# The last chunk of a two-layer kernel cut by groups instead of by tiles, and its last stores on two queues

## The chip, the cores and the metric

The kernel runs on one core of a Trainium2 chip. The metric is the device time of one execution in microseconds (us). The engines are PE (matrix multiply; PEld is its weight load), DVE (vector), ACT (activation), POOL (general purpose) and SP, which here only issues DMAs. ACT can issue DMAs too.

## What is computed

An attention over 12480 tokens of 128 channels with 32 inducing points, and then two layers of 128 to 2048 to 128, the first with `h * cos(h)`, the second with `h * sigmoid(h)`:

```python
h = mab(I, x)                       # 32 points attend to all tokens
x = mab(x, h)                       # all tokens attend to the 32 points
h = x @ w_in;  x = (h * np.cos(h)) @ w_out      # first layer
h = x @ w_in2; out = (h / (1 + np.exp(-h))) @ w_out2   # second layer
```

## The kernel before, in words

The 12480 tokens are seen as 98 tiles: tile t holds for each of 128 partitions one token, and the last tile (t = 97) holds 64 tokens only. The 128 partitions of a tile are four groups g of 32. A run of nt tiles of one group is therefore nt * 32 columns of a matmul; tile 97 exists for groups 0 and 1 alone, so that groups 2 and 3 have 32 columns less there (`width`, L198).

The tiles are cut into seven chunks (L71 to L73): 8 tiles, five times 16 tiles, and the last 10 tiles (88 to 97). The attention of a chunk is done at once; then the chunk's columns are cut into blocks of at most 512 columns (L264 to L272). A full chunk gives four blocks, one group with 16 tiles each. The first and the last chunk are cut by tiles instead: a block takes four tiles (MT) of all four groups. The last chunk thus gives blocks of 512, 512 and 192 columns. There are NB = 25 blocks.

A block goes through both layers in NJ = 8 units; a unit is 256 of the 2048 hidden channels. The kernel has one loop over steps s (L977), written as a software pipeline by hand; step s does for different units:

- `mlp1_in(s)`: 2 matmuls into the PSUM buffer h1 (L768). ACT takes the cosine (L797), DVE multiplies (L801), rounds (L808) and takes the rest (L819).
- `mlp2_in(s - 11)`: 6 matmuls into the single PSUM buffer h2 (L877). ACT does Silu (L892) and rounds (L900), POOL takes the rest (L901). In the last three units the halves of the rounding and of the rest are shared between DVE, ACT and POOL (L903 to L908).
- `mlp2_out(s - 13)`: 6 matmuls (L829) that add up in acc2. After the eighth unit of a block `store` (L921) turns the result on DVE (L924) into the single buffer o and issues its stores on SP (L933, L939).
- `mlp1_out(s - 2)`: 6 matmuls (L829) that add up in acc1; after the eighth unit `y_split` (L857) rounds it on ACT (L862) and takes the rest on DVE (L863).

So a unit costs PE 20 matmuls, whatever the number of its columns. Instructions are issued in the order of the program (a manual schedule), each engine takes its own in that order, and after the last `mlp1_in` 13 more steps drain the pipeline.

`spread` (L289) loads a block's attention weights with DMAs on SP into `stk`: four DMAs for each run of tiles of one group, eight steps ahead of the block. `store` issues for each such run four stores (32 channels each), and one more for a tail tile of groups 0 and 1. A block of one group has one run, a block cut by tiles has four. The last block (tiles 96 and 97 of all groups, 192 columns) thus has 16 stores at L933 and two at L939, in the order: four of group 0, tail of group 0, four of group 1, tail of group 1, four of group 2, four of group 3.

Of the kernel before, what the change touches and what calls it, by code (L numbers as in the profile page):

```python
# [21 lines left out]
def tile_induced_attention_then_two_mlps(  # L22
# [31 lines left out]
    nc = tc.nc  # L54
# [11 lines left out]
    KT = 16  # L66
# [197 lines left out]
    blocks, first_of = [], []  # L264
    for k, (t0, nt) in enumerate(chunks):
        first_of.append(len(blocks))
        if nt == KT:
            blocks += [(k, [(g, t0, nt)]) for g in range(G)]
        else:
            for t in range(t0, t0 + nt, MT):  # L270
                m = min(MT, t0 + nt - t)
                blocks.append((k, [(g, t, m) for g in range(G)]))  # L272
    NB = len(blocks)
# [3 lines left out]
    def places(b):  # L277

        at, out = 0, []
        for g, t, m in blocks[b][1]:  # L280
            n = width((t, m), g)
            out.append((g, t, m, at, n))
            at += n
        return out

    def cols(b):
        return sum(n for *_, n in places(b))
# [459 lines left out]
    def main(general):  # L747
# [173 lines left out]
        def store(b):  # L921
            n = cols(b)
            o = blk.tile([P, KT, Q], F32, tag="o", name="o", bufs=1)
            nc.vector.transpose(  # L924
                o.rearrange("p t d -> p (t d)")[:, 0:n], acc2.pop(b)[:, 0:n]
            )
            ov = out[0 : TF * P, :].rearrange("(p t) c -> p t c", t=TF)
            for g, t, m, at, _ in places(b):
                at //= Q
                full = min(t + m, TF) - t  # L930
                for d in range(G):
                    ds = slice(d * Q, (d + 1) * Q)
                    nc.sync.dma_start(  # L933
                        out=ov[g * Q : (g + 1) * Q, t : t + full, ds],
                        in_=o[ds, at : at + full, :],
                    )
                if full < m and g < GT:
                    r0 = TF * P + g * Q
                    nc.sync.dma_start(  # L939
                        out=out[r0 : r0 + Q, :].rearrange("i (d j) -> d i j", d=G),  # L940
                        in_=o[:, at + full, :],
                    )
# [34 lines left out]
        for s in range(NU + L2 + D2 + 1):  # L977
            if s < NU:
                mlp1_in(s)
            v = s - L2  # L980
            if 0 <= v < NU:
                mlp2_in(v)
            if s < L2:
                out1(s)
            if s < NU:
                mlp1_act(s)
            attend(s, True)
            if 0 <= v < NU:
                mlp2_act(v)
            v = s - L2 - D2  # L990
            if 0 <= v < NU:
                mlp2_out(v)
                if v % NJ == NJ - 1:
                    store(v // NJ)
            if s < NU:
                mlp1_rest(s)
            if s >= L2:
                out1(s)
            attend(s, False)
            more = wait_words or wait_sign or wait_join  # L1000
            if s >= L2:
                words()
            splits(1, 1 if more else 0)
            if s >= PAIRS and wait_pair:
                split(*wait_pair.pop(0))
            fill(s)
# [42 lines left out]
```

## Time and profile before

| | us |
|---|---|
| median of 3 runs | 1006.42 |
| lowest and highest | 1004.85, 1007.32 |
| the profiled execution | 1007.78 |
| its span (first to last instruction) | 1005.9 |

The time of the profiled execution is the span and what lies around it. Starts and lengths in the views are us from the start of the span. A matmul's length holds its way through the array, and matmuls overlap: what a matmul costs in a stream is the distance from one to the next. A row of the chain of waits that merges several matmuls gives such a stream's length. "Granted clock" is the share of TensorE's full clock of 2.4 GHz; 0.5 of it is 1.2 GHz.

### The profile page before, as it was taken

To read this page: it belongs to the slowest core of one execution; us is meant where nothing else is said; L and a number is where in the kernel's file an instruction comes from. 1 tells how busy PE (TensorE), PEld (TensorE's weight loads), DVE (VectorE), ACT (ScalarE), POOL (GpSimd) and SP (SyncE) were. 2 spreads that over 40 slices of the span, in tenths; PEclk is the share of its full clock that TensorE was granted. 3 is DMA by queue.
4 is the path that set the end of the run, shared out by engine and by line. 5 is a ranking of instruction groups with operands and counts; after the bars stand their busy time and mean duration, and the time that the engine had idled before them with its cause. 6 is when DMAs were issued, how large, how long until landed. Compare 5 with 4: busy or idle time off the path is not lost.

```text
span 1005.9 us, 12280 instructions
## 1 busy us (share of the span) xinstructions
PE 972.1 (97%) x4527; PEld 765.3 (76%) x4527; DVE 777.3 (77%) x817; ACT 704.0 (70%) x785; POOL 511.5 (51%) x285
## 2 busy tenths in 40 slices
PE   9987999999999999999999999999999999999993
PEld 6644577788887788887788887788887888888883
DVE  4876588888888888888888888888888888888520
ACT  5778676776766777676777676776767777767662
POOL 2234355555455555555564545555554655454572
PEclk9999999999999999999999999999999999999997
DMA  8431010110010010010010010010010010000001
GB/s 284 131 115 53 22 21 1 21 33 5 17 22 5 16 22 10 13 22 10 11 22 11 12 22 9 12 22 11 11 22 11 11 19 14 11 15 11 1 11 18
DMA packets 67788, 27.93 MB, mean 28 GB/s; under 512 B 55848, under 2 KB 61704, under 8 KB 67720
## 3 DMA queue, kind: packets, MB, share of 16 engines
q1 hardware_dynamic: 67672, 27.06, 11.2%
q8 instruction: 37, 0.61, 0.2%
q14 instruction: 31, 0.25, 0.1%
q10 hardware_dynamic: 48, 0.02, 0.0%
HBM read 14.79 MB, written 6.39 MB: 21 GB/s over the span
## 4 chain that ended last, share of the span: by engine, by line
PE 87%; ACT 3%; DVE 2%; issue 2%; POOL 1%; POOLq 0%; DVEq 0%
PE acc L829 49%; PE h L877 26%; PE h L768 8%; PE acc L839 2%; ACT c L797 1%; ACT L892 1%; ACT s L892 1%; PE s L215 1%; DVE c L801 0%; DVE s2t L226 0%; ACT s2t L236 0%; PE hwps L657 0%; DVE sign L137 0%; DVE sign L132 0%; ACT L236 0%
## 5 line engine op out<-in xcount | busy, mean ns | idle before, releaser
L901 POOL TENSOR_TENSOR lo<-s,hi 128x1024 fp32r<-128x1024 f32 (+1 forms) x189 | 447.4, 2367 | 391.5 <-ACT hi L900 343.7
L829 PE MATMUL acc<-hi,wo 128*128 128x512 f32 (+1 forms) x1504 | 401.6, 389 | 0.2 <-DVE o L924 0.2
L797 ACT ACTIVATE c<-h,half_pi 128x1024 f32<-128x1024 f32 (+1 forms) x200 | 219.0, 1095 | 160.4 <-PE h L768 160.1
L829 PEld LDWEIGHTS acc<-hi,wo 128*128 128x128 f32 x1504 | 279.3, 188 | 60.1 <-issue 1.4
L801 DVE TENSOR_TENSOR h<-h,c 128x1024 f32<-128x1024 f32 (+1 forms) x184 | 221.3, 1203 | 134.2 <-ACT c L797 134.1
L877 PE MATMUL h<-yhi,wi 128*128 128x512 f32 (+1 forms) x800 | 246.5, 390 | 6.3 <-ACT s L892 5.6
L892 ACT ACTIVATE s<-h 128x1024 f32<-128x1024 f32 (+1 forms) x200 | 201.0, 1005 | 69.5 <-PE h L877 67.0
L829 PE MATMUL acc<-lo,wo 128*128 128x512 f32 (+1 forms) x752 | 230.7, 388 | 0.0
L808 DVE CAST hi<-h 128x1024 fp32r<-128x1024 f32 (+1 forms) x184 | 220.0, 1196 | 6.3
L819 DVE TENSOR_TENSOR lo<-h,hi 128x1024 fp32r<-128x1024 f32 (+1 forms) x184 | 219.0, 1190 | 5.5
L900 ACT CAST hi<-s 128x1024 fp32r<-128x1024 f32 (+1 forms) x189 | 195.6, 1035 | 6.1
L877 PEld LDWEIGHTS h<-yhi,wi 128*128 128x128 f32 x800 | 147.6, 188 | 42.4 <-ACT s L892 8.6
L829 PEld LDWEIGHTS acc<-lo,wo 128*128 128x128 f32 x752 | 140.4, 188 | 31.7
L877 PE MATMUL h<-ylo,wi 128*128 128x512 f32 (+1 forms) x400 | 154.8, 387 | 0.0
L768 PE MATMUL h<-stk,hw 128*128 128x512 f32 (+1 forms) x400 | 127.7, 401 | 7.4 <-DVE c L801 6.8
L768 PEld LDWEIGHTS h<-stk,hw 128*128 128x128 f32 x400 | 74.3, 189 | 36.5 <-DVE c L801 12.2
L877 PEld LDWEIGHTS h<-ylo,wi 128*128 128x128 f32 x400 | 75.2, 188 | 15.9
L801 DVE TENSOR_TENSOR c<-h,c 128x1024 f32<-128x1024 f32 x16 | 19.6, 1222 | 19.9 <-ACT c L797 17.8
L839 PE MATMUL acc<-c,wf 128*128 128x512 f32 x64 | 31.2, 612 | 0.9 <-DVE ylo L863 0.9
L863 DVE TENSOR_TENSOR ylo<-acc,yhi 128x512 fp32r<-128x512 f32 (+1 forms) x25 | 16.8, 671 | 12.6 <-ACT yhi L862 12.5
L862 ACT CAST yhi<-acc 128x512 fp32r<-128x512 f32 (+1 forms) x25 | 14.4, 576 | 16.2 <-PE acc L829 13.1
L924 DVE STREAM_TRANSPOSE o<-acc 128x512 f32<-128x512 f32 (+1 forms) x25 | 17.3, 694 | 8.1 <-PE acc L829 8.1
(138 smaller groups left out, 365.8 us busy)
## 6 DMA issues: line engine op xcount, KB each, us to landing
x_sb<-in_x_dram SPq DMA_DIRECT2D x10, 512.0 KB, 6.4
out_dram<-o SPq DMA_DIRECT2D x80, 64.0 KB, 2.0
raw<-in_moe_w_in_dram SPq DMA_DIRECT2D x16, 256.0 KB, 3.3
raw<-in_moe_w_out_dram SPq DMA_DIRECT2D x16, 256.0 KB, 2.8
stk<-ahi SPq DMA_DIRECT2D x40, 64.0 KB, 2.0
stk<-at SPq DMA_DIRECT2D x40, 64.0 KB, 2.0
out_dram<-o SPq DMA_DIRECT2D x66, 16.0 KB, 1.5
x_sb<-in_x_dram SPq DMA_DIRECT2D x3, 192.0 KB, 5.9
```

What stands on the lines that cost most here:

```text
L768: nc.tensor.matmul(ps[:, a, 0:n], lhsT=hw[f // 4][:, f % 4 * P : (f % 4 + 1) * P], rhs=stacks[b][:, 0:n], start=True, stop=True,)
L797: nc.scalar.activation(cs, h, AF.Sin, bias=half_pi, scale=1.0)
L801: nc.vector.tensor_tensor(cs if whole else h, h, cs, ALU.mult)
L808: nc.vector.tensor_copy(hi[:, :, 0:n], h)
L819: nc.vector.tensor_tensor(lo[:, :, 0:n], h, hi[:, :, 0:n].bitcast(F32), ALU.subtract)
L829: nc.tensor.matmul(acc[:, 0:n], lhsT=wt[:, 2 * j + a, :], rhs=gt[:, a, 0:n], start=(j == 0 and p == 0 and a == 0), stop=(j == NJ - 1 and p ...
L839: nc.tensor.matmul(acc[:, 0:n], lhsT=w[:, 2 * j + a, :], rhs=c[:, a, 0:n], start=(j == 0 and a == 0), stop=(j == NJ - 1 and a == 1),)
L877: nc.tensor.matmul(ps[:, a, 0:n], lhsT=wt[:, fs], rhs=yt[:, 0:n], start=(p == 0), stop=(p == 2),)
L892: nc.scalar.activation(sv, hid2.pop(u)[:, :, 0:n], AF.Silu)
L900: nc.scalar.copy(hv, sv)
L901: nc.gpsimd.tensor_tensor(lv, sv, hv.bitcast(F32), ALU.subtract)
L924: nc.vector.transpose(o.rearrange("p t d -> p (t d)")[:, 0:n], acc2.pop(b)[:, 0:n])
```

## The change

The rule that cuts a chunk by groups now holds for every chunk but the first. The last chunk gives four blocks, one group each with tiles 88 to 97: 320 columns for groups 0 and 1, 288 for groups 2 and 3 (NB = 26). In the last block (group 3) the second and fourth of the four stores are issued on ACT's queue instead of SP's.

```diff
@@ -264,7 +264,7 @@
     blocks, first_of = [], []
     for k, (t0, nt) in enumerate(chunks):
         first_of.append(len(blocks))
-        if nt == KT:
+        if k > 0:
             blocks += [(k, [(g, t0, nt)]) for g in range(G)]
         else:
             for t in range(t0, t0 + nt, MT):
@@ -930,7 +930,8 @@
                 full = min(t + m, TF) - t
                 for d in range(G):
                     ds = slice(d * Q, (d + 1) * Q)
-                    nc.sync.dma_start(
+                    queue = nc.scalar if b == NB - 1 and d % 2 else nc.sync
+                    queue.dma_start(
                         out=ov[g * Q : (g + 1) * Q, t : t + full, ds],
                         in_=o[ds, at : at + full, :],
                     )
```

## Rows read from the trace of the kernel before

**Rows 1.** The page's busy times: engine, us, share of the span, instructions.

```profile
PE 972.1 (97%) x4527; PEld 765.3 (76%) x4527; DVE 777.3 (77%) x817; ACT 704.0 (70%) x785; POOL 511.5 (51%) x285
```

**Rows 2.** The chain of waits in order of time: start us, us, what, count.

```profile
51.55 1.91 PE st L712 x15
...
875.78 0.45 PE h L768 x2
876.23 1.37 PE h L877 x6
877.61 2.77 PE acc L829 x12
...
982.26 0.67 PE acc L829 x6
```

**Rows 3.** Windows: stretch, its us, busy us of each engine, granted clock, DMA, GB/s.

```profile
965.89:990.71 24.82, 24.63 (x158) 21.34 (x156) 2.93 (x8) 14.34 (x24) 16.66 (x12) 1.00 0.08 12
...
991.10:1005.90 14.80, 0.00 (x0) 0.00 (x0) 0.00 (x0) 0.00 (x0) 0.00 (x0) 0.59 0.07 12
```

**Rows 4.** The timeline of the end: start us, us, engine, line, operation, count.

```profile
990.71 0.38 DVE L924 STREAM_TRANSPOSE o<-acc 128x192 f32<-128x192 f32 x1 [0.90 <-PE acc L829]
991.12 2.92 SPq L933 DMA_DIRECT2D out_dram<-o  x4
...
998.34 3.71 SPq L933 DMA_DIRECT2D out_dram<-o  x8
```

**Rows 5.** Groups by line and shape: count | busy us, mean ns | idle before, releasers.

```profile
L797 ACT ACTIVATE c<-h,half_pi 128x1024 f32<-128x1024 f32 x192 | 214.4, 1117 | 158.5 <-PE h L768 158.5
L892 ACT ACTIVATE s<-h 128x1024 f32<-128x1024 f32 x192 | 197.1, 1027 | 64.4 <-PE h L877 63.4 <-POOL lo L901 0.9
L900 ACT CAST hi<-s 128x1024 fp32r<-128x1024 f32 x184 | 193.0, 1049 | 5.9
...
L797 ACT ACTIVATE c<-h,half_pi 128x384 f32<-128x384 f32 x8 | 4.7, 583 | 1.9 <-PE h L768 1.6
L892 ACT ACTIVATE s<-h 128x384 f32<-128x384 f32 x8 | 3.9, 491 | 5.1 <-PE h L877 3.6 <-POOL lo L901 1.5
L900 ACT CAST hi<-s 128x384 fp32r<-128x384 f32 x5 | 2.6, 513 | 0.2
...
L801 DVE TENSOR_TENSOR h<-h,c 128x1024 f32<-128x1024 f32 x176 | 216.8, 1232 | 124.0 <-ACT c L797 124.0
L801 DVE TENSOR_TENSOR h<-h,c 128x384 f32<-128x384 f32 x8 | 4.5, 565 | 10.2 <-ACT c L797 10.1
...
L901 POOL TENSOR_TENSOR lo<-s,hi 128x1024 fp32r<-128x1024 f32 x184 | 442.4, 2404 | 389.4 <-ACT hi L900 341.6 <-issue 40.9 <-PE h L768 6.9
L901 POOL TENSOR_TENSOR lo<-s,hi 128x384 fp32r<-128x384 f32 x5 | 5.0, 1007 | 2.1 <-ACT hi L900 2.1
```

**Rows 6.** DMA issues: timeline rows of SP and ACT, then sizes and us to landing.

```profile
921.90 1.95 SPq L933 DMA_DIRECT2D out_dram<-o  x4
...
0.73 0.40 ACTq L323 DMA_DIRECT2D ind_sb<-in_inducing_dram  x1
...
out_dram<-o SPq DMA_DIRECT2D x80, 64.0 KB, 2.0
...
out_dram<-o SPq DMA_DIRECT2D x16, 4.0 KB, 1.6
...
DMA to landing us min/median/max: 1.4/1.8/3.8
```

**Rows 7.** The timeline of one step of the drain, 192 columns.

```profile
983.54 0.27 PE L877 MATMUL h<-ylo,wi 128*128 128x192 f32 x1
...
983.91 0.49 ACT L892 ACTIVATE s<-h 128x384 f32<-128x384 f32 x1 [0.52 <-PE h L877]
...
984.46 0.36 PE L877 MATMUL h<-yhi,wi 128*128 128x192 f32 x1
```

**Rows 8.** Groups by line and shape: PE's matmuls into h2.

```profile
L877 PE MATMUL h<-yhi,wi 128*128 128x512 f32 x768 | 240.3, 394 | 6.3 <-ACT s L892 5.6 <-DVE s2t L226 0.7
```

## The prediction

> **What bounds the kernel now.** I read the busy table first, then the windows, the chain, and last SP's queue at the end. PE is busy for 97% of the span [rows 1], and up to the last stores the chain is made of matmuls [rows 2]. The reader should see two things. First, a step of the steady pipeline is 2 + 6 + 12 = 20 matmuls and takes 0.45 + 1.37 + 2.77 = 4.59 us without a gap, 0.230 us per matmul of 512 columns. Second, the span does not end with the matmuls. The last transpose starts at 990.71; from 991.10 to 1005.90 PE, DVE, ACT and POOL do nothing at all [rows 3]. In that stretch SP issues the last block's stores [rows 4]: eighteen in all (four groups of four, and two stores of the tail rows), the first at 991.12, the last done at 998.34 + 3.71 = 1002.05. No row shows SP waiting between them. The issuing, 10.9 us, is the path, and 3.85 us follow from the last issue to the end of the span.
>
> The profiled execution took 1007.78 us around a span of 1005.9; it is 1.36 us above the median of 1006.42. I make the sum on its span and take the difference off the median.
>
> **Part 1: the last block's stores.** The blocks of the last chunk are now one group each, so the last block has one run of tiles in the output and four stores, and as it is group 3 it has no tail store (those two move to the blocks of groups 0 and 1, earlier). The odd two of the four go to ACT's queue. Removed: fourteen issues and the tail stores at the end. Cost of the new end: the transpose of 288 columns instead of 192. DVE's operations grow by (1.232 - 0.565)/640 = 1.04 ns per element [rows 5], so 0.38 + 0.10 = 0.48 us. Then 0.03 us to the first issue, and two issues on SP. Eight in a row took 3.71 us [rows 4], 0.46 each; four stores of 64 KB, the larger form, took 1.95 us, 0.49 each [rows 6], so size hardly counts: 0.95 us. ACT's one DMA issue took 0.40 us [rows 6]; ACT has nothing behind it at this point, and its two run beside SP's. Then the 3.85 us. The part of these that is landing may grow: 4 KB landed in 1.6 us and 64 KB in 2.0 us [rows 6], so a store of 36 KB adds 0 to 0.4 us; I take 0.2, the middle, as 36 KB lies midway. New end: 0.48 + 0.03 + 0.95 + 3.85 + 0.2 = 5.5 us after the transpose starts, where it was 1005.9 - 990.71 = 15.2 us. **Part 1: -9.7 us.**
>
> If the four were all on SP, two more issues would cost 0.95 us; that alone is what the second queue is worth by these rows. The page DMA: Bandwidth & Descriptors of the Trainium skill (section Issuing engines are not separate DMA queues) says that issuing from several engines saves only the sequencer's issue time, usually small beside the transfer. By that rule the second queue gives nothing; here issuing is 10.9 us beside landings of 1.6, so the trace makes the sequencer the thing that counts.
>
> **Part 2: the matmuls of the last chunk.** Before: two blocks of 512 columns and one of 192. After: two of 320 and two of 288; the same 1216 columns, eight more units, 160 more matmuls. A block is 8 units of 20 matmuls. Six matmuls of 192 columns take 0.67 us, 0.111 each [rows 2]. Before: 320 x 0.230 + 160 x 0.111 = 91.4 us. The trace has no full-array matmul of 320 or 288 columns, so I bound it by the nearest rows. Upper end: a straight line from 192 to 512 (0.372 ns per column) gives 0.159 and 0.147 us, 320 x 0.306 = 97.7, **+6.3 us**. Lower end: in proportion to the columns from 512, 0.144 and 0.129, 87.4 us, **-4.0 us**. Between them: fifteen matmuls of 128 columns take 1.91 us [rows 2]; without the 0.28 us of the last one that is 0.116 us each, no less than at 192. So 192 sits on a floor, and the line drawn from it is too flat. The granted clock is 1.00 here [rows 3], the level of 2.4 GHz. With one column per clock and a fixed rest (an estimate), 512 columns are 0.213 + 0.017, so 320 are 0.150 and 288 are 0.137, both above the floor: 320 x 0.287 = 91.7 us. I take this: **+0.3 us**. The overhead of 160 extra matmuls is paid by the 160 that no longer sit on the floor.
>
> The page TensorE: Matmul & The Clock Gate (section Back-to-back issue gap) gives columns/2.4 + 2.5 ns for an isolated warm matmul; by it the new blocks would take 82.7 us. The trace does not agree: at 512 columns it has 0.230 us where the page has 0.216, and at 192 it has 0.111 where the page has 0.083.
>
> **Part 3: the other engines in these steps.** Per unit ACT does three operations. From 1024 and 384 elements [rows 5] they cost 0.80 + 0.71 + 0.73 = 2.23 us at 640, and 2.07 at 576; PE's step is 20 x 0.150 = 3.00 and 2.73. DVE does three, 0.83 each at 640, 2.5 us, and 2.3 at 576. POOL's one costs 1.57 and 1.43. All hide behind PE, DVE with the least room (83% busy, as now in the steady stretch). The cover is a full PE; where PE is not full, in the drain, it is gone. The 48 loads of stk for this chunk become 16, issued eight steps ahead: nothing.
>
> **Part 4: the drain.** After the last unit has entered, only the second layer runs. From 965.89 to 990.71 there are 24.8 us [rows 3], of which matmuls are 48 x 0.230 + 108 x 0.111 = 23.0, so 1.8 us are waits. Each step waits for the one h2 buffer: from the start of the last matmul into h2 (983.54) to the Silu (983.91), 0.49 us of Silu, to the next first matmul at 984.46 [rows 7], 0.92 us against 7 x 0.111 = 0.78 of own work. With 288 columns the way back is 0.37 + 0.04 + 0.65 + 0.06 = 1.12 against 7 x 0.137 = 0.96: 0.16 us instead of 0.14. The end chain (Silu, halves of the split, the last matmuls) grows by some 0.4 us. Waits 1.8 + 0.2 + 0.3 = 2.3 us. **Part 4: +0.4 us**, so that the transpose starts at 990.71 + 0.3 + 0.4 = 991.4.
>
> **Sum:** +0.3 + 0.4 - 9.7 = -9.0 us; span 996.9, this execution 998.8, median 1006.42 - 9.0 = **997.4 us**. A measurement of this kernel can tell some 0.3%, 3.0 us, from no change.
>
> **The rivals.**
> *A, cheap columns.* Spacing goes down in proportion: 4.3 us less than my sum, 993.1. For it: nothing direct; against it: the floor at 128 and 192 shows a part that does not shrink. Chance 0.10.
> *B, dear columns.* The straight line: 6.0 us more, 1003.4, which is just 0.3% below before. For it: the only two sizes on a full array that the steps have; against: the 128-column row. Chance 0.08, half of it within 0.3%.
> *C, the second queue does not run beside the first* (ACT issues late or its stores land late; this is the case where that part does not do what it says, and the case of the page's rule). At least the two issues come back, 0.95 us, and if a store on ACT's queue lands like the slowest of the stores, 3.8 us against a median of 1.8 [rows 6], 2 us on top: 998.4 to 1000.4. For it: ACT issues nothing since the first microsecond, so no row shows its queue late in the run. Against: nothing else is queued on ACT. Chance 0.13.
> *D, slower: the single h2 buffer becomes the bound of the short steps.* PE has 14 matmuls between filling h2 and filling it again, 2.1 us at 320 and 1.9 at 288. Silu alone comes back in 1.1 to 1.2 us. If ACT's order puts the cosine (0.80) in front of it, 1.95: about even. If the split's cast (0.73) stands there as well, 2.68, which is 0.6 to 0.8 us too late in each of some 27 two-layer steps, 18 us: 1015. It decides from the point where Silu starts more than 1.2 us after h2 is full. Against: at 512 columns ACT waits for PE before Silu for 63.4 us in all [rows 5] while PE waits for Silu 5.6 us in all [rows 8], and the ratio of ACT's work to PE's step rises only from 0.69 to 0.76. Chance 0.04.
>
> **How the numbers follow.** Main case 0.65; A 0.10, C 0.13, B 0.08, D 0.04. Faster by over 0.3%: main, A, C, half of B, less 0.01 for a sum of small waits, about 0.91; slower: D, 0.03 of it beyond the bound; the rest, 0.06, within. The range reaches from 994.0 (most of A, and the low bound of the column price) to 1002.0 (C, and two thirds of B's extra); left out are D, half of B and the outer part of A.
>
> **What would show it.** Right: after the last transpose SP has two stores of about 0.46 us and ACT two beside them, and the span ends some 5.5 us after the transpose starts; the steps of 320 columns take 3.0 us and those of 288 take 2.7 without gaps on PE; the last transpose starts near 991.4. Wrong: steps of 3.2 us with no PE gaps (B), PE waiting for the Silu in two-layer steps (D), stores on ACT that start or land over 1 us after SP's (C). My sum fails if the 3.85 us after the last issue are not a fixed end but grow when less stands before them.

## The result and the profile after

The changed kernel takes 997.65 us (median of 4 runs, 996.65 to 999.07) against 1006.5 us beside it: a ratio of 0.9915, 95% interval 0.9896 to 0.9934, 8.9 us less; by the interval it is 6.6 to 10.5 us less. The forecast was 997.4 us, 9.0 us less. The profiled execution took 998.4 us around a span of 996.6. The total is right to a few tenths; two of its terms are each off by 1.5 us or more, in opposite directions.

The last chunk's matmuls. The chain of waits, in order of time, columns as in [rows 2]: first a step in which both layers work on 320 columns, then one with both on 288, then one of the drain.

```profile
918.68 0.30 PE h L768 x2
918.98 0.87 PE h L877 x6
919.86 1.76 PE acc L829 x12
...
960.83 0.26 PE h L768 x2
961.09 0.79 PE h L877 x6
961.88 1.59 PE acc L829 x12
...
982.05 1.07 PE h L877 x6
983.11 0.79 PE acc L829 x6
```

A step is 20 matmuls in 2.93 us at 320 columns, 0.147 each, and in 2.64 us at 288, 0.132 each; no piece lies between them, so PE stays the bound. In the drain, 6 matmuls into h2 take 1.07 us instead of 0.79: the wait for Silu is inside. For comparison a step of the drain before, where six matmuls without a wait take 0.67 us:

```profile
982.93 0.88 PE h L877 x6
983.82 0.67 PE acc L829 x6
```

The windows of the changed kernel show the same by sums (columns as in [rows 3]): the last chunk from its first matmul to the end of the step with the last one that enters the first layer, the drain, and the stretch behind the last transpose.

```profile
861.78:966.12 104.34, 104.34 (x643) 98.04 (x642) 80.14 (x104) 78.47 (x100) 59.57 (x33) 1.00 0.07 12
966.12:989.63 23.51, 23.00 (x156) 20.68 (x155) 4.82 (x9) 14.24 (x23) 15.57 (x12) 1.00 0.05 8
990.12:996.60 6.48, 0.00 (x0) 0.00 (x0) 0.00 (x0) 0.00 (x0) 0.00 (x0) 0.78 0.20 34
```

And the first of these in the kernel before, which [rows 3] continue with the 24.82 us of its drain:

```profile
861.84:965.89 104.05, 104.05 (x481) 86.23 (x480) 76.72 (x79) 73.47 (x75) 57.44 (x24) 1.00 0.07 11
```

From the chunk's first matmul to the last transpose it was 104.05 + 24.82 = 128.87 us and is 104.34 + 23.51 = 127.85: **1.02 us less**. The chunk's first matmul is the mark to compare from. Nothing is changed ahead of it, yet in the ten profiles it lies between 859.9 and 863.6 us; most of the difference is there by the first matmul of the first layer (52.3 to 54.8). Spans of two single profiles differ by that much for no reason of the change.

The end. The timeline, columns as in [rows 4]:

```profile
989.63 0.48 DVE L924 STREAM_TRANSPOSE o<-acc 128x288 f32<-128x288 f32 x1 [1.16 <-PE acc L829]
990.15 1.92 SPq L934 DMA_DIRECT2D out_dram<-o  x2
990.15 1.91 ACTq L934 DMA_DIRECT2D out_dram<-o  x2
```

The two queues do run side by side, from 990.15 on. But two issues take 1.92 us where eight took 3.71 [rows 4], and from the last issue to the end there are 996.6 - 992.07 = 4.5 us instead of 3.85. From the start of the last transpose to the end it is 7.0 us, where it was 15.2: **8.2 us less**, and not the 9.7 of the forecast.

The view of the DMA issues in the stretch from 990.1 to 992.2 (columns as in [rows 6]) has the landings close together:

```profile
out_dram<-o SPq DMA_DIRECT2D x2, 36.0 KB, 2.7
out_dram<-o ACTq DMA_DIRECT2D x2, 36.0 KB, 3.0
```

The other engines, by shape (columns as in [rows 5]), and DVE with the least room:

```profile
L797 ACT ACTIVATE c<-h,half_pi 128x640 f32<-128x640 f32 x16 | 12.7, 795 | 7.6 <-PE h L768 7.5
L892 ACT ACTIVATE s<-h 128x640 f32<-128x640 f32 x16 | 11.3, 705 | 2.7 <-PE h L877 1.9
L801 DVE TENSOR_TENSOR h<-h,c 128x640 f32<-128x640 f32 x16 | 13.3, 833 | 14.4 <-ACT c L797 14.4
L901 POOL TENSOR_TENSOR lo<-s,hi 128x576 fp32r<-128x576 f32 x13 | 18.6, 1429 | 11.4 <-ACT hi L900 10.4 <-PE acc L829 0.9
```

These are the prices worked out from [rows 5] (0.80, 0.71, 0.83 and 1.43 us) to the hundredth. ACT still waits for PE ahead of Silu and ahead of the cosine.

### The profile page after: what moved, and what is told of

It is laid out like the page before. It is cut to its first block, busy times and chain, and to the rows that moved or that the text cites. A ratio compares the mean times of both kernels' runs of the same rounds, so it can differ in the third digit from the quotient of the medians.

```text
span 996.6 us, 12618 instructions
## 1 busy us (share of the span) xinstructions
PE 970.7 (97%) x4687; PEld 775.5 (78%) x4687; DVE 782.6 (79%) x843; ACT 708.7 (71%) x810; POOL 512.7 (51%) x293
## 4 chain that ended last, share of the span: by engine, by line
PE 88%; ACT 3%; issue 2%; DVE 2%; POOL 1%; POOLq 0%; DVEq 0%; ACTq 0%
PE acc L829 49%; PE h L877 27%; PE h L768 8%; PE acc L839 3%; ACT c L797 1%; ACT L892 1%; ACT s L892 1%; PE s L215 1%; DVE c L801 0%; DVE s2t L226 0%; ACT s2t L236 0%; PE hwps L657 0%; ACT L236 0%; DVE sign L137 0%; DVE sign L132 0%
## 5 line engine op out<-in xcount | busy, mean ns | idle before, releaser
L901 POOL TENSOR_TENSOR lo<-s,hi 128x1024 fp32r<-128x1024 f32 (+2 forms) x197 | 447.9, 2274 | 389.1 <-ACT hi L900 343.0
L829 PE MATMUL acc<-hi,wo 128*128 128x512 f32 (+2 forms) x1568 | 403.0, 379 | 0.0
L797 ACT ACTIVATE c<-h,half_pi 128x1024 f32<-128x1024 f32 (+2 forms) x208 | 221.1, 1063 | 158.0 <-PE h L768 157.9
L801 DVE TENSOR_TENSOR h<-h,c 128x1024 f32<-128x1024 f32 (+2 forms) x192 | 222.7, 1160 | 132.6 <-ACT c L797 132.3
L877 PE MATMUL h<-yhi,wi 128*128 128x512 f32 (+2 forms) x832 | 248.0, 380 | 6.7 <-ACT s L892 5.9
L892 ACT ACTIVATE s<-h 128x1024 f32<-128x1024 f32 (+2 forms) x208 | 202.3, 973 | 66.1 <-PE h L877 64.4
L829 PE MATMUL acc<-lo,wo 128*128 128x512 f32 (+2 forms) x784 | 232.8, 378 | 0.1
L808 DVE CAST hi<-h 128x1024 fp32r<-128x1024 f32 (+2 forms) x192 | 221.2, 1152 | 6.6
L819 DVE TENSOR_TENSOR lo<-h,hi 128x1024 fp32r<-128x1024 f32 (+2 forms) x192 | 220.2, 1147 | 5.7
L900 ACT CAST hi<-s 128x1024 fp32r<-128x1024 f32 (+2 forms) x197 | 196.6, 998 | 6.3
```

Of the source, the lines that this page charges most:

```text
L797: nc.scalar.activation(cs, h, AF.Sin, bias=half_pi, scale=1.0)
L801: nc.vector.tensor_tensor(cs if whole else h, h, cs, ALU.mult)
L808: nc.vector.tensor_copy(hi[:, :, 0:n], h)
L819: nc.vector.tensor_tensor(lo[:, :, 0:n], h, hi[:, :, 0:n].bitcast(F32), ALU.subtract)
L829: nc.tensor.matmul(acc[:, 0:n], lhsT=wt[:, 2 * j + a, :], rhs=gt[:, a, 0:n], start=(j == 0 and p == 0 and a == 0), stop=(j == NJ - 1 and p ...
L877: nc.tensor.matmul(ps[:, a, 0:n], lhsT=wt[:, fs], rhs=yt[:, 0:n], start=(p == 0), stop=(p == 2),)
```

## The experiments

**1. The second queue taken back.** All four last stores on SP:

```diff
-                    queue = nc.scalar if b == NB - 1 and d % 2 else nc.sync
-                    queue.dma_start(
+                    nc.sync.dma_start(
```

> The changed kernel with all four last stores on SP. Theory (each issue costs SP 0.46 us, and one of them 1.5 us because the instruction fetch at the end of the loop falls on it): SP takes about 2.9 us for the four where it now takes 1.92 for two, and the end comes 0.95 us later, span about 997.5. Rival (two queues issuing at once are what makes the second issue long): four issues in 1.9 us, no later end, span 996.6. Second rival (nothing gained by the second queue, since the end is set by something else than SP): SP later by 1 us, end unchanged.

999.87 us (4 runs), ratio 0.9931, interval 0.9914 to 0.9948, which overlaps that of the whole change: the runs alone can't tell the two apart. The profile (span 996.9) shows where they differ. Its timeline at the end, whole and then issue by issue:

```profile
989.43 0.48 DVE L924 STREAM_TRANSPOSE o<-acc 128x288 f32<-128x288 f32 x1 [1.16 <-PE acc L829]
989.94 2.72 SPq L933 DMA_DIRECT2D out_dram<-o  x4
...
990.30 0.46 SPq L933 DMA_DIRECT2D out_dram<-o  x1
...
990.80 1.36 SPq L933 DMA_DIRECT2D out_dram<-o  x1
...
992.20 0.46 SPq L933 DMA_DIRECT2D out_dram<-o  x1
```

Four issues take 2.72 us, 0.8 more than the 1.92 of two. From the chunk's first matmul to the end it is 135.3 us against 134.8 with two queues: in this one pair of profiles the second queue is worth **0.5 us**, half of the 0.95 expected, as the stretch behind the last issue is 0.3 us shorter here. The first rival falls: a long issue is there with one queue too, only it is the third now. Against the second rival, an unchanged end, there are these 0.5 us alone.

**2. The second queue alone, on the old blocks.**

```diff
-                    nc.sync.dma_start(
+                    queue = nc.scalar if b == NB - 1 and d % 2 else nc.sync
+                    queue.dma_start(
```

> The kernel before with its old blocks, and only the second half of the change: the odd ones of the last block's sixteen stores on ACT. The last transpose stays at 990.7. Theory (the two sequencers issue side by side): SP has ten of eighteen left, eight at 0.46 and up to two at 1.5 us, 6 to 7 us instead of 10.9, span about 1002, ACT done before SP. Rival (issues of the two queues go one after the other behind the sequencers): 10.9 us as before, span 1005.9.

1003.16 us (10 runs) against 1007.06, ratio 0.997, interval 0.9958 to 0.9983; the medians are 3.9 us apart. The profile has a span of 1001.3 with the transpose at 989.10. Some rows of its end:

```profile
989.51 6.62 ACTq L934 DMA_DIRECT2D out_dram<-o  x8
991.39 0.70 SPq L940 DMA_DIRECT2D out_dram<-o  x1
...
994.23 2.97 SPq L934 DMA_DIRECT2D out_dram<-o  x4
```

SP is done at 997.20, 7.7 us after its first issue instead of 10.9, so the queues issue side by side, and ACT is done first, at 996.13. The 7.7 us are more than the 6 to 7 expected: both queues stand still for 1.4 us before 995.8, where each waits on the semaphore of the store eight before it (eight go round both queues). From the chunk's first matmul to the end it is 141.1 us against 144.1 before, and the interval of the ratio holds 1.7 to 4.2 us. So the queue is worth some 3 us where eighteen stores stand at the end, and 0.5 where four do; the two halves of the change do not add up.

**3 and 4. No last stores.** In both kernels:

```diff
+            if b == NB - 1:
+                return
```

> The changed kernel without the last block's four stores (left out: the output of group 3's last ten tiles). Theory (the 3.85 to 4.5 us after the last issue are a fixed end of every program, not the landing of the stores): the span ends 3.9 to 4.4 us after the last transpose's end, about 994.2. Rival (they are the landing): the span ends within 2 us of the transpose, below 992.5.

> The kernel before without the last block's eighteen stores (left out: the output of tiles 96 and 97). With the run without last stores of the changed kernel it prices the new blocks alone. Theory: last transpose at 990.7, span about 995.2, 1.0 us more than the other run, so that the blocks alone are worth 1.0 us and the stores the other 8.2. Rival (the blocks are worth nothing or cost time, as forecast): the two spans differ by less than 0.3 us or the other way.

Spans of 991.9 and 996.0. The last transposes and the spans:

```profile
core 0 of [0], span 991.9 us
987.80 0.48 DVE L924 STREAM_TRANSPOSE o<-acc 128x288 f32<-128x288 f32 x1 [1.16 <-PE acc L829]
```
```profile
core 0 of [0], span 996.0 us
991.48 0.38 DVE L924 STREAM_TRANSPOSE o<-acc 128x192 f32<-128x192 f32 x1 [0.91 <-PE acc L829]
```

With no store left the program still ends 3.6 us after the transpose with the new blocks, and 4.1 with the old ones: most of what follows the last issue is not the landing of the stores. The theory's range was 3.9 to 4.4; the rival's bound was 2. The span of 991.9 is below the 992.5 that the rival gave, but only because the whole run is shifted. What leaves the loop last there is PE: the trace has its branch out of the loop at 3.67 and 4.03 us, and the end 0.9 us behind it. The spans differ by 4.1 us, but 2.7 of that is the start of the chunk (859.93 and 862.60 us). From that mark the two differ by 1.4 us: the 1.02 to the last transpose, which both runs repeat (127.87 and 128.89 us), and 0.4 behind it. The 0.4 can't be put down to the blocks: it is the length of PE's branch, which in the ten profiles lies between 3.5 and 4.25 us with either kind of block. The last stores cost 144.08 - 133.41 = 10.67 us before and 134.83 - 131.99 = 2.84 us after, 7.83 us less; with the 1.4 us that is the whole of the 9.25 us between the two kernels from that mark.

**5. PE leaves the loop later.** Eight matmuls behind the last one, their result not used:

```diff
+        for _ in range(8):
+            nc.tensor.matmul(
+                spin[:, 0, :], lhsT=wi2[0][:, 0:P], rhs=wi2[1][:, 0:512], start=True, stop=True
+            )
```

> The changed kernel with eight matmuls of 512 columns added on PE behind the last one (nothing waits for them), so that PE leaves the loop, and its fetch of the code behind the loop starts, some 1.8 us later. Theory (the 1.5 us issue is long because that fetch runs at the same time): the second issue of both queues comes down to about 0.45 us, or the long one moves to whatever is issued then; SP and ACT are done by 1.0 us after the first issue. Rival (the second issue on a queue is long by itself, or because two queues issue): still 1.5 us.

998.06 us, span 996.3; the second issues take 1.53 and 1.46 us. The run decides nothing: the trace has PE's branch out of the loop at 989.25 us, when the array was still to run the eight matmuls, and the 16 KB fetch of instructions that follows at 990.3 us, where the changed kernel has it at 990.1. PE's sequencer goes ahead of the array, so work put behind the last matmul does not hold it.

**6. The drain without the single buffer.** The units that enter h2 after the last unit of the first layer take the two buffers of h1:

```diff
-            ps = psh.tile([P, 2, 512], F32, tag="h2", name="h2")
+            late_h = u + L2 >= NU
+            ps = psh.tile([P, 2, 512], F32, tag="h1" if late_h else "h2", name="h2", bufs=2 if late_h else 1)
```

> The changed kernel with the units of the drain (those filled after the last unit of the first layer) taking the two h1 buffers, which are free by then, instead of the single h2. Theory (each drain step waits for Silu to give h2 back): the steps go from 1.86 to 12 matmuls of 0.132 us, 1.58, and the last transpose comes 2.2 us earlier, 24.0 instead of 26.2 us after the last matmul of the first layer's input. Rival (ACT's 1.33 us and POOL's 1.43 us a step with their waits are the bound right behind): less than 1 us.

995.09 us (4 runs), ratio 0.9892, interval 0.9876 to 0.9909; span 992.8. The chain in the drain, and the same two windows as above:

```profile
980.65 0.79 PE h L878 x6
981.44 0.79 PE acc L829 x6
982.23 0.80 PE h L878 x6
```
```profile
860.37:964.71 104.34, 104.34 (x643) 98.03 (x642) 80.14 (x104) 78.47 (x100) 59.57 (x33) 1.00 0.07 12
964.71:985.82 21.11, 20.95 (x156) 20.42 (x155) 4.85 (x9) 14.21 (x23) 15.75 (x12) 1.00 0.05 9
```

The drain steps are 1.58 us, and the drain takes 21.11 instead of 23.51 us, 2.4 less. So the steps' waits were for the one buffer, and neither ACT nor POOL becomes the bound. Of the kernels here that write the whole output this one is the fastest, 2.6 us under the change by the medians; their intervals overlap, and it is the windows that show the 2.4.

**7. A third size on the curve.** The kernel before, with its last chunk cut by two tiles a block instead of four:

```diff
-            for t in range(t0, t0 + nt, MT):
-                m = min(MT, t0 + nt - t)
+            step = 2 if k else MT
+            for t in range(t0, t0 + nt, step):
+                m = min(step, t0 + nt - t)
```

> The kernel before with its last chunk still cut by tiles, but two tiles a block: four blocks of 256 columns and the one of 192, with the old eighteen last stores. It puts a third size on the curve of the matmul's price. Theory (one column per clock above a floor of 0.111 us, with the rest seen at 288 and 320): 0.118 to 0.120 us at 256 columns, 94 us of matmuls against 91.4, and 3 to 5 us more in all, from the chunk's first matmul to the last transpose 132 to 134 us instead of 128.9. Rival (the straight line between 192 and 512): 0.135 us, 104 us of matmuls, 141 us or more.

1010.18 us, span 1008.3; 131.4 us from the chunk's first matmul to the last transpose, a little under the 132 to 134 expected. A step of 256 columns in its chain:

```profile
938.46 0.23 PE h L769 x2
938.69 0.71 PE h L878 x6
939.40 1.42 PE acc L830 x12
```

20 matmuls in 2.36 us, 0.118 each: the theory's lower end. The curve is 0.111 (192 columns), 0.118 (256), 0.132 (288), 0.147 (320), 0.230 (512). At 256 columns the floor, 0.111, already is nearly all of the price, and 1216 columns cost 2.5 us more than before although each block is smaller. The straight line of rival B is far off.

**8. The last stores later.** Seven copies on DVE ahead of the last transpose:

```diff
+            if b == NB - 1:
+                late = u1.tile([P, 2, W], F32, tag="c", name="c", bufs=2)
+                for _ in range(7):
+                    nc.vector.tensor_copy(late[:, 0, 0:n], acc2[b][:, 0:n])
```

> The changed kernel with seven copies of acc2 on DVE (their result is not used) ahead of the last transpose, so that its stores are issued some 2.3 us later, while PE and its fetch of the code behind the loop stay where they are. Theory (an issue that meets the 16 KB instruction fetch is long, whichever it is in its queue): the first fetch, which took 1.2 to 1.5 us from about 0.5 us after the last matmul's start, is over by then, the two issues of each queue take 0.3 to 0.45 us, 0.85 in all instead of 1.92, unless they now meet the second fetch some 3.5 us after the first. Rival (the second issue on a queue is long because of the first one's 288 pieces): still 1.9 us for two.

1002.83 us. The copies took 3.4 us instead of 2.3, so the stores met the second of the two fetches, and SP's and ACT's second issues came out apart. The issues, one by one:

```profile
995.26 0.32 SPq L938 DMA_DIRECT2D out_dram<-o  x1
995.27 0.38 ACTq L938 DMA_DIRECT2D out_dram<-o  x1
...
995.62 0.60 SPq L938 DMA_DIRECT2D out_dram<-o  x1
...
995.69 1.58 ACTq L938 DMA_DIRECT2D out_dram<-o  x1
```

SP's second issue is 0.60 us and ACT's second 1.58, with the same pieces behind the same kind of first store. The 16 KB fetch of instructions began at 995.74 us and took 1.10. The rival falls: the second issue is not long by itself. At the end of every profile with last stores the trace has such a fetch where an issue is long; six of them:

| run | 16 KB fetch: start, length | long issues: start, length |
|---|---|---|
| before | 991.81, 1.32; 995.88, 0.96 | SP 991.96, 1.62; SP 995.77, 1.43 |
| after | 990.09, 1.48 | SP 990.50, 1.56; ACT 990.57, 1.49 |
| one queue | 990.47, 1.19 | SP 990.80, 1.36 |
| queue alone | 989.79, 1.12 | SP 989.89, 1.46; ACT 989.93, 1.42 |
| drain on h1 | 986.29, 1.18 | SP 986.69, 1.28; ACT 986.75, 1.22 |
| late stores | 995.74, 1.10 | ACT 995.69, 1.58 |

The first issue after a pause goes through in 0.32 to 0.38 us even during a fetch, and so does one that was well under way when the fetch began (0.46 us at 990.30 with one queue); the next one is long. Where it ends says more than that it overlaps: in the ten traces 74 issues take 0.8 us or more, 67 of them overlap a 16 KB fetch, and each of the 67 ends 0.2 to 0.5 us after the fetch does. The rule has exceptions. Seven long issues (0.8 to 1.2 us) have no such fetch. SP's 0.60 above began 0.11 us ahead of its fetch, as did the 1.43 at 995.77 in the kernel before. In the run with two tiles the second fetch (997.28, 1.39 us) holds an issue of 0.57 us from start to end; the next takes 0.85.

The view of the DMA queues lists these fetches as "q8 instruction" (packets, MB, share of the 16 engines); in the run with one queue, for the stretch from 990.30 to 990.77, just ahead of the long issue:

```profile
q8 instruction: 1, 0.02, 15.8%
```

No run took the fetch away, so that it makes the issues long is borne out by where they begin and end in ten traces, not by its removal.

## Why the prediction was right, and where not

**What bounds the kernel: right.** The end was SP's issuing. Without its last stores the kernel before ends 10.7 us earlier (from the chunk's mark), and with four stores of the new form it ends 8.2 us sooner behind the transpose. Without the rows of SP's queue, one would have looked for the gain on PE, where it is 1.0 of the 9.3 us by which the spans differ.

**Part 1, forecast -9.7, measured -8.2: the mechanism right, the size off.** The step that failed is "two issues on SP. Eight in a row took 3.71 us [rows 4], 0.46 each", 0.95 us in all: they took 1.92. The price was read from the eight issues at the very end, the only undisturbed row; among the first ten of the eighteen two were long (1.62 and 1.43 us), and the first row of SP in [rows 4], four in 2.92 us, showed it, 0.73 each. All four issues of the shorter list begin within the time of the fetch. The second failed step is "then the 3.85 us" with 0.2 for the landing: it is 4.5 us. It is the point that the forecast named as its weak one. And it is not landing: the last store has landed at 993.76 us, 1.6 us before SP's next instruction, as in the kernel before. From SP's branch out of the loop to that next instruction it is 3.17 us, and 2.49 before; that is the whole difference. Why it is longer stays open. In the four profiles in which a 16 KB fetch begins in that stretch it is 2.8 to 3.2 us, in the four in which none does 2.5 to 2.7; but in three of the first four ACT also leaves the loop within 0.03 us of SP, and no run separates the two.

**The second queue.** Forecast 0.95 us, by rows 0.5 us in the profile. The page DMA: Bandwidth & Descriptors of the Trainium skill (section Issuing engines are not separate DMA queues) says that a second issuing engine saves only the sequencer's time, usually small beside the transfer. The traces agree on what is saved: 10.9 us of issuing before, 7.7 with the queue alone. One issue, 0.46 us, is small beside its landing, 1.8; but landings overlap and issues on one queue do not, so that for eighteen stores the issuing is the larger.

**Part 2, forecast +0.3, measured -2.3: right in kind, too dear.** The step is "a fixed rest" of 0.017 us added to one clock per column. By the steps it is 0.013 at 320 columns and 0.012 at 288: 320 x (0.1465 + 0.132) = 89.1 us instead of 91.7, against 91.4 before. Of rival A it has a good half; the floor and the kink stand, as the run with 256 columns shows. The formula for an isolated matmul on the page TensorE: Matmul & The Clock Gate of the Trainium skill (section Back-to-back issue gap) gives, as an estimate, 0.136 and 0.123 us for these sizes; the trace does not agree, it has 0.01 more each.

**Part 3: right.** The prices by shape came out to 0.01 us and stayed hidden.

**Part 4, forecast +0.4, measured +1.1.** By its own terms, waits of 2.3 us instead of 1.8, the forecast should have been +0.5. The drain took 23.5 us, of which matmuls are 156 x 0.132 = 20.6; so waits are 2.9 us and not 2.3. The failed step is "0.16 us instead of 0.14" a step: a step is 1.86 us against 1.58 of matmuls, 0.28 us, which is 0.05 more than in the old drain, whose step took 1.56 us against 12 x 0.111. The larger part is the number of such steps, which the forecast left as it was: in the old chain four steps wait (from 982.93 to 987.59), in the new one eight (from 972.74 to 985.77). In the old drain the steps that still held matmuls of 512 columns show no such wait; now the block ahead of the last has 288 columns too. Against that, a wait of 0.8 us for the transpose of the block ahead (979.89 to 980.68 in the old chain) is gone. That the wait is the single h2 is shown by the run that gives the drain two buffers.

**The sum.** -2.3 + 1.1 - 8.2 = -9.4 us where the spans differ by 9.3. The errors of Part 1 (+1.5), Part 2 (-2.6) and Part 4 (+0.7) cancel to -0.4; that 997.4 came within 0.3 us of the median is luck, as each of these errors alone is larger. **Rivals:** B and D fell, B by 0.147 and 0.132 us, D by a chain without a gap in the two-layer steps. C fell as stated (ACT's stores issue together with SP's and land 0.2 and 0.3 us later), though its price, 1 to 3 us at the end, holds the 1.5 us by which the end was missed for other reasons.

## What to carry to other kernels

Read the end of the span as a stage of its own: once the engines stop, every DMA issue on one queue is path, and a list of small stores is cheaper as a few larger ones than on a second queue. A price taken from a merged row should come from the part of the row that the changed list will stand in, here the first four issues and not the last eight. When blocks get smaller, put the price of a matmul on a curve with a floor, and look in the drain for the single buffer that two stages no longer cover: giving it a second one here was worth 2.4 us more.

## What the runs showed of the hardware

- A DMA issue at a 16 KB instruction fetch often takes 0.8 to 2.1 us instead of 0.42 to 0.6, on SP and on ACT alike, and then ends 0.2 to 0.5 us after the fetch does (67 issues in ten traces); long issues in the middle of the kernel before fall on such fetches too (at 213.92 us 1.69, at 625.51 us 1.97, each with a fetch within 0.25 us). No run removed the fetch.
- PE's sequencer leaves the loop while the array still has eight matmuls, 2 us of work, to run.
- With no DMA left to wait for, the program still needs 3.6 to 4.1 us from its last transpose's end to the end of the span; with stores, the last of them has landed 1.6 us before SP's next instruction, before and after the change.
- The last chunk, behind the same first 176 units, starts up to 3.6 us earlier or later from one profile to the next, and 2.5 us of it are there before the first layer begins.
